# A hand-ordered kernel for linear attention and a feed-forward block: a new order of steps, more transposes by DMA, wider warm matmuls

## The chip, the cores and the metric

The kernel runs on one core of one Trainium2 chip. The metric is the device time of one execution in microseconds; lower is better. Before the change it is 157.49 us, the median of three runs (156.46 to 158.19).

## What is computed

The first part is linear attention with a decaying state, for 4 batches, 8 heads, 768 positions and head dimension 48. Its output, 384 wide, is the input x of the second part: a normalisation over the 384 columns, a matmul to 1536, a relu, a matmul back to 384, and x added.

```python
def _attn_ref(r, k, v, w, u):
    ...
    for t in range(S):
        kt, vt, rt = (k[:, :, t].copy(), v[:, :, t].copy(), r[:, :, t].copy())
        cur = np.einsum('bhd,bhe->bhde', u[None] * kt, vt)
        y[:, :, t] = np.einsum('bhd,bhde->bhe', rt, state + cur)
        state = w[None, :, :, None] * state + np.einsum('bhd,bhe->bhde', kt, vt)

def _moe_ref(x, g_ln, w_ch1, w_ch2):
    mu = np.mean(x, axis=-1, keepdims=True)
    var = np.mean((x - mu) ** 2, axis=-1, keepdims=True)
    xn = (x - mu) / np.sqrt(var + 1e-06) * g_ln
    ch = np.maximum(xn @ w_ch1, 0.0) @ w_ch2
    return (x + ch).astype(np.float32)
```

All inputs and the output are float32.

## The kernel before

The work is cut into 24 chunks of 128 positions (6 for each batch); chunks of one batch hand a state Z on from one to the next. Every piece of work on a chunk is a small function with a short name, and a table written out in the source, PLAN, lists some 1,100 steps in the form name, index, engine (v for VectorE, DVE; s for ScalarE, ACT; g for GpSimd, POOL). The program calls them in the order of the table. No scheduler moves anything: each engine executes its own steps in the table's order, and a step that waits holds everything behind it on its engine. The SyncE queue (SP) is such an order, too. It issues nearly all DMAs, and one that waits for its data or for a free buffer holds all later ones.

The steps of the start-up:

- WF loads the row w, LG the gains; LN, WBM (a matmul that spreads the row), FK and FR make the decay factors Fk and Fr of keys and rows from it. ROWSI issues four small loads of u and w from ACT's queue; UW (POOL) and WL (ACT) make from them what S and ZU need.
- MW and MP fill constants and the padding of key and row tiles, on DVE.
- LW1 n loads a third of the first weight matrix (768 KB), SW i scales a ninth of it into bf16 (three steps for each third), IW2 n loads a third of the second matrix; it is issued by POOL.
- WU and DU are matmuls on a zero tile that compute nothing; their index is how many.

The steps of chunk i:

- LK, LR, LV load keys, rows (r) and values, 192 KB each, in ten buffers each. SK and SR multiply keys and rows by their factors, CV casts the values.
- TR transposes scaled rows and keys on PE, eight transposes, into the PSUM tile `tr`, which has one buffer; TC (or TCr and TCk) copies them out. In TKD a DMA turns the keys, in TRD the rows; then TR has four transposes, or isn't there.
- AT makes the attention scores, AM (or AMa and AMb) multiplies them by the mask on DVE. Q multiplies turned rows and keys for the diagonal. S makes the diagonal sums and the chunk's contribution to the state, CC copies the sums out, ZU and ZD update the state, VB multiplies values by the sums, Y makes the output of the attention in PSUM, and X adds both to x on DVE.
- SQ and XN give square sums and the centred x, RS the factor of the normalisation. LT transposes xn on PE into `tr` and XT copies it out; for later chunks LTD does both by DMA.

Chunks 0 to 7 and 20 to 23 enter the feed-forward part alone, chunks 8 to 19 in pairs (GROUPS). UP of index 16 g + m makes up to 512 columns of the hidden layer of group g, RL is its relu, DN of index 4 i + d adds a third of the second matmul of chunk i, OT adds x, STO stores. The last chunk is done in halves (DA, DB, OA, OB, SA, SB).

Of the kernel before, what the change touches and what calls it, by code (L numbers as in the profile page):

```python
# [92 lines left out]
def kernel(  # L93
# [105 lines left out]

    def times(e, out, in0, in1):  # L200
        engines[e].tensor_tensor(out=out, in0=in0, in1=in1, op=ALU.mult)  # L201
# [429 lines left out]
```

## Time and profile before

| What | Value |
|---|---|
| Median of three runs | 157.49 us |
| Span of the profiled execution, first to last instruction | 153.7 us |
| TensorE (PE), busy | 143.1 us, 93% |
| VectorE (DVE), busy | 106.4 us, 69% |
| ScalarE (ACT), busy | 88.7 us, 58% |
| GpSimd (POOL), busy | 87.5 us, 57% |
| DMA packets, bytes | 93142, 25.53 MB |
| of these packets, under 512 B | 88385 |
| HBM read and written | 18.88 MB, 4.72 MB |

The profiled execution's own time is known by its span; the 3.8 us between 153.7 and the median of the runs lie around it (start and end of the program). In a row of the timeline the first two numbers are the start and the length in us; in a group of instructions, the numbers behind the bar are busy time in us, mean duration in ns, and the idle time of the engine before them with what ended it. PE counts as busy while its pipeline drains, so a PE that is 93% busy can still start its matmuls late.

### The profile page before, as it was taken

What the parts mean: (1) busy time and instruction counts of PE and PEld (TensorE: products, weight loads), DVE (VectorE), ACT (ScalarE), POOL (GpSimd) and SP (SyncE); (2) the same over time, 40 slices, a digit from 0 to 9 for tenths busy, and PEclk for the clock granted to TensorE, in tenths of its full rate; (3) what the DMA queues carried; (4) which work ended last, traced back from release to release, by engine and by line L of the source; (5) the groups of instructions that cost most, each with busy time, mean ns of one, the idle gap of its engine ahead of it and who ended that gap; (6) DMA issues with size and microseconds to landing.
All of it is one profiled execution on the core that took longest, in us unless ns stands there. A gap on an engine that the chain in (4) does not pass through costs nothing.

```text
span 153.7 us, 4643 instructions
## 1 busy us (share of the span) xinstructions
PE 143.1 (93%) x1866; PEld 115.1 (75%) x1866; DVE 106.4 (69%) x220; ACT 88.7 (58%) x190; POOL 87.5 (57%) x126
## 2 busy tenths in 40 slices
PE   7989696999999999899999999999999999899991
PEld 4877585877786788688678769688787887568880
DVE  3399785655998886958884969997887454455121
ACT  4424794436648857667868657638577444144440
POOL 3437697422575897485932899573843969431100
PEclk9999999999999999999999999999999999999999
DMA  3999999949999897989988999595353754212211
GB/s 48 212 214 353 208 306 211 200 108 219 226 198 246 167 230 164 209 168 214 231 198 174 258 201 187 109 188 115 81 152 85 123 163 114 53 51 78 80 51 51
DMA packets 93142, 25.53 MB, mean 166 GB/s; under 512 B 88385, under 2 KB 91586, under 8 KB 93122
## 3 DMA queue, kind: packets, MB, share of 16 engines
q1 hardware_dynamic: 91858, 24.06, 71.2%
q0 software_dynamic: 432, 1.18, 3.9%
q8 instruction: 14, 0.23, 0.6%
q10 hardware_dynamic: 832, 0.00, 0.3%
q14 instruction: 6, 0.05, 0.1%
HBM read 18.88 MB, written 4.72 MB: 154 GB/s over the span
## 4 chain that ended last, share of the span: by engine, by line
PE 54%; DMA 21%; DVE 9%; SPq 6%; issue 3%; POOL 3%; ACT 1%; DVEq 0%; ACTq 0%; POOLq 0%
PE o L527 22%; PE hp L499 21%; DMA kf<-in_k_dram 11%; DMA w_sb<-in_moe_w_ch_dram 4%; DVE A L365 3%; DMA vf<-in_v_dram 3%; DMA xT<-xn 3%; PE at L355 2%; PE tr L336 2%; SPq L320 2%; POOL Vb L418 2%; PE y L436 2%; SPq L317 2%; PE s L399 1%; PE y L428 1%
## 5 line engine op out<-in xcount | busy, mean ns | idle before, releaser
L515 ACT ACTIVATE hT<-hp 128x512 bf16<-128x512 f32 x70 | 41.2, 596 | 32.2 <-PE hp L499 31.1
L499 PE MATMUL hp<-xT,w_sb 128*128 128x128 bf16 (+1 forms) x648 | 57.0, 237 | 1.6 <-DMA xT<-xn 0.8
L527 PE MATMUL o<-w_sb,hT 128*128 128x384 bf16 x276 | 53.9, 326 | 2.0 <-DMA w_sb<-in_moe_w_ch_dram 1.1
L499 PEld LDWEIGHTS <-w_sb 128*128 128x128 bf16 x648 | 49.0, 114 | 5.9 <-DMA xT<-xn 1.1
L527 PEld LDWEIGHTS <-hT 128*128 128x128 bf16 x276 | 24.8, 98 | 14.1 <-DMA w_sb<-in_moe_w_ch_dram 1.3
L365 DVE TENSOR_TENSOR A<-at,mask 128x1024 bf16<-128x1024 f32 (+1 forms) x26 | 29.4, 1135 | 0.9 <-PE at L355 0.7
L418 POOL TENSOR_TENSOR Vb<-vf,cc 128x384 f32<-128x384 f32 x24 | 20.2, 841 | 13.6 <-ACT cc L196 7.6
L583 DVE SCALAR_TENSOR_TENSOR ot<-o,rs,x 128x384 f32<-128x384 f32 x23 | 14.1, 613 | 16.8 <-PE o L527 14.6
L450 ACT ACTIVATE sqj<-x,sm 128x384 bf16<-128x384 f32 x24 | 14.7, 613 | 4.2 <-DVE x L443 3.9
L443 DVE SCALAR_TENSOR_TENSOR x<-y,Vb 128x384 f32<-128x384 f32 x24 | 13.2, 552 | 4.6 <-POOL Vb L418 2.7
L201 POOL TENSOR_TENSOR sck<-kf,Fk 128x384 bf16<-128x384 f32 x10 | 10.0, 1008 | 9.3 <-DMA kf<-in_k_dram 6.3
L201 POOL TENSOR_TENSOR scr<-rf,Fr 128x384 bf16<-128x384 f32 x9 | 9.8, 1091 | 8.8 <-DVE q L201 5.1
L201 POOL TENSOR_TENSOR q<-trs 128x512 bf16<-128x512 bf16 x9 | 10.9, 1215 | 6.7 <-DVE trs L198 4.0
L201 POOL TENSOR_TENSOR Z<-ZS,WLZ 128x384 bf16<-128x384 f32 x12 | 12.0, 1004 | 2.3 <-DVE ZS L412 2.3
L196 ACT COPY trs<-tr 128x1024 bf16<-128x1024 bf16 (+1 forms) x12 | 10.4, 866 | 3.2 <-PE tr L336 3.2
L201 DVE TENSOR_TENSOR sck<-kf,Fk 128x384 bf16<-128x384 f32 x14 | 8.1, 582 | 5.9 <-DMA kf<-in_k_dram 5.6
L201 DVE TENSOR_TENSOR q<-trs 128x512 bf16<-128x512 bf16 x15 | 9.1, 604 | 4.2 <-ACT trs L196 3.3
L467 POOL TENSOR_TENSOR rs<-rs,expo 128x1 f32<-128x1 f32 (+1 forms) x18 | 10.8, 602 | 1.5
L355 PE MATMUL at<-trs 48*128 48x128 bf16 x192 | 9.5, 218 | 0.5 <-DVE trs L198 0.4
L201 DVE TENSOR_TENSOR scr<-rf,Fr 128x384 bf16<-128x384 f32 x15 | 8.8, 599 | 1.8 <-DMA rf<-in_r_dram 1.6
L196 ACT CAST vv<-vf 128x384 bf16<-128x384 f32 x16 | 8.2, 510 | 3.1 <-DMA vf<-in_v_dram 2.3
L259 PE MATMUL o<-warm 128*128 128x128 bf16 x94 | 8.9, 261 | 1.0 <-DVE warm L224 1.0
(72 smaller groups left out, 176.2 us busy)
## 6 DMA issues: line engine op xcount, KB each, us to landing
rf<-in_r_dram SPq DMA_DIRECT2D x24, 192.0 KB, 3.7
kf<-in_k_dram SPq DMA_DIRECT2D x24, 192.0 KB, 4.0
vf<-in_v_dram SPq DMA_DIRECT2D x24, 192.0 KB, 3.8
out_dram<-ot SPq DMA_DIRECT2D x23, 192.0 KB, 2.1
w_f<-in_moe_w_ch_dram SPq DMA_DIRECT2D x3, 768.0 KB, 6.5
w_sb<-in_moe_w_ch_dram POOLq DMA_DIRECT2D x3, 384.0 KB, 7.9
out_dram<-ot SPq DMA_DIRECT2D x2, 96.0 KB, 1.6
trs<-sck SPq DMA_TRANSPOSE x10, 2.9
```

The source lines that it names most:

```text
L196: nc.scalar.copy(out=out, in_=in_)
L201: engines[e].tensor_tensor(out=out, in0=in0, in1=in1, op=ALU.mult)
L355: nc.tensor.matmul(out=t[:, par, q, :], lhsT=trs(i)[p0 : p0 + D, 1, q, :], rhs=trs(i)[p0 : p0 + D, 0, q, :], start=True, stop=True,)
L365: nc.vector.tensor_tensor(out=AA(i)[:, a:b].rearrange("p e q t -> p (e q) t"), in0=psum["at", i][:, a:b].rearrange("p e q t -> p (e q) t") ...
L418: nc.gpsimd.tensor_tensor(out=Vb(i)[:].rearrange("p (h d) -> p h d", h=H), in0=vf(i)[:], in1=cc(i)[:].unsqueeze(2).to_broadcast([P, H, D]) ...
L443: nc.vector.scalar_tensor_tensor(out=xx(i)[:], in0=psum["y", i][:, :C], scalar=1.0, in1=Vb(i)[:], op0=ALU.mult, op1=ALU.add, accum_out=sm[ ...
L450: nc.scalar.activation(out=sqj[:], in_=xx(i)[:], func=ACT.Square, bias=sm[i][:], scale=-float(C), accum_out=sq[g][:, j : j + 1])
L467: nc.gpsimd.tensor_tensor(out=rs[g][:], in0=rs[g][:], in1=expo[:, :n], op=ALU.pow)
L499: nc.tensor.matmul(out=t[:, a * gw : (a + 1) * gw], lhsT=w1_sb[n][kc][:, fb::FB], rhs=xT(g)[:, kc, :gw], start=(kc == 0), stop=(kc == CK - 1),
L515: nc.scalar.activation(out=o, in_=s, func=ACT.Relu)
L527: nc.tensor.matmul(out=psum["o", i][:, :C], lhsT=hT(g)[:, fk, j * P : (j + 1) * P], rhs=w2_sb[d][:, a, :], start=(fk == 0), stop=(fk == FK ...
L583: nc.vector.scalar_tensor_tensor(out=ot(i)[:], in0=psum["o", i][:, :C], scalar=rs[g][:, j : j + 1], in1=xx(i)[:], op0=ALU.mult, op1=ALU.add,)
```

## The change

The table PLAN is replaced as a whole. Order, engines and the number of DU matmuls are new. Keys are turned by DMA from chunk 12 on (before 14), r from chunk 18 (before 20), xn from chunk 12 (before 14). VB and ZD take their engine from the table (before always POOL). WU and DU use one matmul of 512 columns for four of 128, by reading the zero tile four times. Stores can be issued by ACT, which this table doesn't use.

By the tables, these counts change (v, s, g):

| Step | Before | After |
|---|---|---|
| RL | v 2, s 70 | v 20, s 52 |
| VB | g 24 | v 8, g 16 |
| ZD | g 12 | v 7, g 5 |
| Q | v 15, g 9 | v 18, g 6 |
| SK | v 14, g 10 | v 11, g 13 |
| SR | v 15, g 9 | v 12, g 12 |
| XN | v 8, s 12, g 4 | v 4, s 14, g 6 |
| CV | v 3, s 16, g 5 | v 5, s 14, g 5 |
| SW | v 3, s 4, g 2 | v 2, s 6, g 1 |
| TKD, TRD, LTD | 10, 4, 10 | 12, 6, 12 |
| WU and DU, in 128 columns | 94 | 105 |

```diff
-K_BY_DMA = [14, 15, 16, 17, 18, 19, 20, 21, 22, 23]
+K_BY_DMA = [12, 13, 14, 15, 16, 17, 18, 19, 20, 21, 22, 23]
...
 PLAN = """
-MW,0,v WF,0,- TL,0,s MI,0,g WU,13,- MM,0,g MP,0,v LN,0,s LG,0,- ROWSI,0,s WBM,0,- LR,0,-
-UGC,0,s FK,0,s LK,0,- FR,0,s LR,1,- SR,0,g WL,0,s SK,0,v LK,1,- UW,0,g DU,24,- TR,0,-
-SR,1,v LK,2,- TCk,0,v SK,1,v LV,0,- TCr,0,v SK,2,v DU,12,- AT,0,- LR,2,- TR,1,- CV,0,s
-AMa,0,v LV,1,- Q,0,g AMb,0,v SR,2,v LW1,0,- DU,7,- Y,0,- S,0,- TCk,1,v CC,0,s TCr,1,v
-CV,1,s ZU,0,v Q,1,g DU,10,- TR,2,- LV,2,- TC,2,v DU,4,- AT,1,- VB,0,g S,1,- SW,2,s
-AMa,1,v LW1,1,- SW,1,g SW,0,s X,0,v Q,2,v CV,2,g XN,0,s AMb,1,v DU,20,- LT,0,- CC,1,v
-SQ,0,s Y,1,- ZU,1,v LK,3,- VB,1,g AT,2,- XT,0,v SW,5,s SW,4,v RS,0,g UP,0,- LR,3,-
-X,1,v SW,3,s AM,2,v S,2,- SK,3,g XN,1,s LW1,2,- UP,1,- RL,0,s SR,3,v LT,1,- IW2,0,g
-SQ,1,s Y,2,- XT,1,v IW2,1,g RL,1,s CC,2,v DU,1,- TR,3,- ZU,2,v VB,2,g UP,17,- LV,3,-
-TC,3,s SW,8,g UP,16,- X,2,v RL,17,s SW,7,v IW2,2,g AT,3,- SW,6,v RL,16,s CV,3,g Q,3,v
-DU,3,- UP,18,- SQ,2,s XN,2,g UP,2,- AM,3,v RS,2,g RL,18,s LT,2,- DN,0,- RS,1,g XT,2,v
-S,3,- RL,2,s UP,34,- CC,3,v VB,3,g Y,3,- RL,34,s ZU,3,v UP,32,- DN,1,- X,3,v UP,33,-
...
+MW,0,v TL,0,s MM,0,g LK,0,- WU,13,- DU,32,- MI,0,g LV,0,- LG,0,- WF,0,- LV,1,- LR,0,- LK,1,- LK,3,- LN,0,s WBM,0,-
+DU,20,- LR,1,- LK,2,- FR,0,s LW1,1,- FK,0,s SR,0,v LR,2,- ROWSI,0,s MP,0,v SK,0,g LW1,2,- TR,0,- DU,8,- SR,1,v SK,1,v
+CV,1,s LR,3,- TCk,0,v UGC,0,s TCr,0,s Q,0,v TR,1,- AT,0,- DU,8,- TCk,1,v CV,0,v LV,2,- AMa,0,v WL,0,s UW,0,g LW1,0,-
+SR,2,v SW,5,s S,0,- DU,16,- AMb,0,v SW,4,g LV,3,- TCr,1,s CC,0,v SK,2,g SK,3,v LK,4,- SW,8,s ZU,0,v LR,4,- Q,1,v
+SW,6,v S,1,- VB,0,v Y,0,- TR,2,- CC,1,s SW,3,s SR,3,g X,0,v AT,1,- DU,8,- TC,2,s AMb,1,v CV,2,g AMa,1,v XN,0,s
+VB,1,g LK,5,- ZU,1,v SW,1,s Y,1,- IW2,0,g Q,2,v LT,0,- X,1,v LR,5,- S,2,- IW2,1,g XT,0,v AT,2,- SW,0,v CC,2,s
+CV,3,s UP,1,- LV,4,- AM,2,v XN,1,g SW,2,s TR,3,- VB,2,g LR,6,- TC,3,s ZU,2,v Y,2,- SK,4,g LK,6,- UP,0,- X,2,v
+LT,1,- Q,3,v XN,2,s SR,4,v S,3,- RL,1,s XT,1,v AT,3,- RL,0,s LT,2,- SR,5,v UP,17,- SQ,0,s XT,2,v AM,3,v TR,4,-
+SQ,1,s RS,0,g UP,16,- RL,17,s SK,5,v IW2,2,g DN,0,- SW,7,s CC,3,v LK,7,- TC,4,v VB,3,g UP,32,- RL,16,v Y,3,- RL,32,s
+TR,5,- X,3,v UP,18,- LR,7,- Q,4,v SQ,3,s ZU,3,v CV,4,g AT,4,- TC,5,s LR,8,- UP,2,- AM,4,v SR,6,g S,4,- RL,18,s
...
+    def issuer(e):
+        return nc.scalar if e == "s" else nc.sync
...
     def WU(i, e):
         if not warm_ps:
             warm_ps.append(ps.tile([P, 512], FP32, name="o"))
-        for _ in range(i):
+        wide, rest = divmod(i, 4)
+        for _ in range(wide):
+            nc.tensor.matmul(
+                out=warm_ps[0][:], lhsT=warm[:], rhs=warm[:].unsqueeze(1).to_broadcast([P, 4, P]), start=True, stop=True
+            )
+        for _ in range(rest):
             nc.tensor.matmul(out=warm_ps[0][:, :P], lhsT=warm[:], rhs=warm[:], start=True, stop=True)
...
     def ZD(i, e):
-        times("g", ZZ(i)[:], ZS(i)[:], WLZ[:])
+        times(e, ZZ(i)[:], ZS(i)[:], WLZ[:])
 
     def VB(i, e):
-        nc.gpsimd.tensor_tensor(
+        engines[e].tensor_tensor(
             out=Vb(i)[:].rearrange("p (h d) -> p h d", h=H), in0=vf(i)[:],
             in1=cc(i)[:].unsqueeze(2).to_broadcast([P, H, D]), op=ALU.mult,
         )
...
     def STO(i, e):
         b, c = divmod(i, NCH)
-        nc.sync.dma_start(out=out[b, c * L : (c + 1) * L, :], in_=ot(i)[:])
+        issuer(e).dma_start(out=out[b, c * L : (c + 1) * L, :], in_=ot(i)[:])
```

In the new table the loads and DMA turns on SP begin LK 0, LV 0, LG 0, WF 0, LV 1, LR 0, LK 1, LK 3, LR 1, LK 2, LW1 1, LR 2, LW1 2, LR 3, LV 2, LW1 0, LV 3, LK 4, LR 4, LK 5, LR 5, LV 4, LR 6, LK 6, LK 7, LR 7, LR 8; the first store, STO 0, stands behind LR 9 (before behind LK 5). In the middle of the table TKD 12 stands behind LK 15, and LK 18 behind TKD 12.

## Prediction

> **What bounds the kernel now.** I read the engines' busy shares and the slices first, then the chain of waits, then the timeline of the first 30 us, then the groups by shape.
>
> ```profile
> span 153.7 us, 4643 instructions
> ...
> PE   7989696999999999899999999999999999899991
> ...
> DMA  3999999949999897989988999595353754212211
> ```
>
> TensorE (PE) is full from slice 8 on, the DMA engines until about 95 us. So two limits follow each other: arriving data, then PE's own work.
>
> ```profile
> 10.62 7.57 DMA kf<-in_k_dram
> 18.32 0.94 POOL sck L201
> 19.26 6.73 DMA w_sb<-in_moe_w_ch_dram
> 26.04 0.82 PE o L527 x4
> ...
> 63.92 4.95 DMA kf<-in_k_dram
> ...
> 128.88 3.89 DMA xT<-xn
> ```
>
> Columns: start, length. The start-up waits for keys 3, which hold POOL and thereby the issue of the first w2 block; DN 0 starts at 26.04. At 63.92 keys arrive late again, and at 128.88 one transposed row block.
>
> ```profile
> 1.03 1.57 PE L259 MATMUL o<-warm 128*128 128x128 bf16 x13 [1.03 <-DVE warm L224]
> 2.09 0.52 ACT L265 ACTIVATE ln_row<-w_row 1x384 f32<-1x384 f32 x1
> 2.10 0.93 ACTq L213 DMA_DIRECT2D u_p<-in_u_dram  x2
> 3.05 0.96 ACTq L213 DMA_DIRECT2D w_p<-in_w_dram  x2
> 4.24 2.74 PE L259 MATMUL o<-warm 128*128 128x128 bf16 x24
> 4.41 0.58 ACT L273 ACTIVATE Fk<-y,pow_i 128x384 f32<-128x384 f32 x1
> 13.80 1.28 PE L259 MATMUL o<-warm 128*128 128x128 bf16 x20
> 17.06 0.86 PE L499 MATMUL hp<-xT,w_sb 128*128 128x128 bf16 x12
> ```
>
> Row w arrives by 2.09, Fk starts at 4.41, the first UP at 17.06. A warm matmul of 128 columns costs 107 ns at first (24 start within 2.5 us) and 56 ns later (20 in 1.1).
>
> **My measure: lag.** From start to start PE spends 0.67 us on a single UP, 0.655 on a paired one, 0.65 on DN, 0.33 on half a DN, 0.22 on four transposes, 0.33 on AT, 0.17 on LT, 0.20 on Y and 0.10 on S, with 0.17 more on each for 20 chunks. With 36 single and 36 paired UP, 69 DN, 6 halves, 34 times four transposes, 24 AT, Y and S and 14 LT, all such work is 127.0 us before. Lag is the time minus the work done up to there; it can only grow, and each growth is a wait of PE (or a warm matmul): 16.4 at DN 0 (9.7 done), 23.3 at the last matmul's end (150.33). So the dense part loses 6.9: about 2.0 until 57 us, 3.1 from there to 82, 1.8 later. Behind PE lie 3.4 us of span, and 3.8 from the span to the runs' median (157.49).
>
> **The change, part by part.** *PE work.* Keys 12, 13 and rows 18, 19 leave PE (4 x 0.22), the normalised rows of 12 and 13 too (2 x 0.17): 1.2 off, 125.8 remain. The six DMA turns that replace them cost SP 1.2 us of issue each and land after 2.9. LTD stands further from its UP now (Y to UP: at least 8.5 us of PE work for chunks 12 to 22, against 4.4), and the turns of keys 12 and 13 have 5 us of PE work before AT, so I take 0; the shortest is keys 22 with 2.9. Uncovered, one costs what LTD 21 cost, 0.9. On SP, keys 18 and values and rows 16 queue behind TKD 12, which waits for SK 12; their users stand 15 us of PE work later.
>
> *Row w* goes from first to fourth on SP, behind keys 0 and values 0. The first load took 3.15 us to land (issued 1.61), each next one 0.9. So keys 0 land at 0.73 + 3.15 = 3.9 and values 0 at 4.8; I take row w at 4.4, between (3.6 if nothing delays it: fourth issue at 2.3, and the 1.36 it took before; 5.4 if both must land first), 2.3 late.
>
> *Warm matmuls* in 512 columns have the same columns: 105 times 128 against 94, 0.6 us more at 56 ns, under waits for data. But 45 of them now precede WBM: 1.03 + 45 x 0.107 = 5.85, then WBM 1.6 (two passes, as before). Fr and Fk run from 7.6 to 8.7, 3.2 late. Should PE speed up at 4.9 instead, they come 0.6 earlier, and the next load hides it.
>
> *ROWSI* moves behind Fk on ACT. Its four issues take 1.9 us there (2.10 to 4.01), now 8.7 to 10.6; CV 1, UGC and TCr 0 queue behind, so Q 0 starts at 11.9. The rows land 3.5 after the last issue, at 13.7: UW, so S 0, and WL, so ZU 0, wait for that.
>
> *DVE's start.* MP (0.9) now stands behind SR 0. SR 2 waits for rows 2, the ninth load, behind one w1 block; before, the same volume had landed at 14.76 (values 2), and the first load now goes out 0.8 earlier: 14.0. Then DVE runs without a pause: SR 2, AMb, CC, SK 3, ZU, Q 1 are 2.5; SW 6 needs the second w1 block (17.5 - 0.8 = 16.7); SW 6, VB 0, X 0, two masks, ZU 1, Q 2, X 1, XT 0 are 4.3. First UP at 21.0, where 4.2 of PE's work is done; before it was 17.06 at 3.8. Start-up lag grows from 13.3 to 16.8.
>
> *Loads against w2.* POOL reaches IW2 0 at 20.0 (rows 3, the tenth load, at 18.19 - 0.8 = 17.4; then SR 1.1, CV 0.7, VB 0.8). Before, packets followed the issue by 2.8 us, one block took 2.0, and while they ran the loads nearly stood: keys 4 landed at 24.31, the next load at 30.68. Twelve loads and three w1 blocks had landed by 22.23; now by 21.4, then keys 4 and rows 4 by 23.2. Blocks 0 and 1 run from 22.8 to 26.8 and leave keys 5 and rows 5 behind: 26.8 + 2 x 0.9 + 0.6 to land = 29.2. DVE has SR 5 ahead of XT 2, and TR 4 needs the PSUM bank that XT 2 frees: TR 4 at 30.1 instead of after UP 17 (26.0), with 8.1 done. **Lag 22.0**, 5.6 more than at DN 0 before. Low bound: loads keep half the queue, rows 5 at 26.9, lag 19.7; high: with 1.8 of a cold PE, 23.8. The third w2 block, behind RS 0 on POOL, goes out at 27 and lands by 35; DN 2 needs it at 16.8 + 22.0 = 38.8, so it costs nothing.
>
> *Engines.* Eighteen RL go to DVE, eight VB and seven ZD leave POOL for it.
>
> ```profile
> L515 ACT ACTIVATE hT<-hp 128x512 bf16<-128x512 f32 x70 | 41.2, 596 | 32.2 <-PE hp L499 31.1
> L517 DVE TENSOR_SCALAR hT<-hp 128x512 bf16<-128x512 f32 x2 | 1.4, 688 | 0.4 <-PE hp L499 0.4
> L418 POOL TENSOR_TENSOR Vb<-vf,cc 128x384 f32<-128x384 f32 x24 | 20.2, 841 | 13.6 <-ACT cc L196 7.6 <-DVE cc L198 5.9
> L201 DVE TENSOR_TENSOR sck<-kf,Fk 128x384 bf16<-128x384 f32 x14 | 8.1, 582 | 5.9 <-DMA kf<-in_k_dram 5.6
> ```
>
> Start to start a RL on DVE is 0.61; VB and ZD there are unseen, nearest is SK, 0.47 (bounds: 0.41, the fastest xn, and 1.2, the slowest SR). Summed so (mask 1.14, OT 0.53, X 0.48, ZU 0.46, Q 0.43, RL on ACT 0.49, VB 0.79 and ZD 0.96 on POOL), DVE goes from 98 to 111 us, ACT from 76 to 69, POOL from 82 to 72. From X 3 to X 8 DVE has 23.3 us against 24.8 of PE work; before, against 30.7. DVE is nearly a second bound there. Both engines wait for each other in turn (AT, mask, Y, x, LT, UP), but the mask stands 2 to 5 us ahead of its Y as before; so I keep the early loss of 2.0. [...] In this trace 13 of 14 SK on DVE take about 0.55, also under POOL's work, and one 0.99. [...]
>
> *The middle* improves. The first store stood behind keys 5 and held SP for 4.3 us; it now follows rows 9. Keys 12 landed at 68.87 when 49.9 of PE work preceded their use (69.0 - 49.9 = 19, the lag itself). The new order asks for the loads nearly in order of use; after rows 5 the tightest is rows 7, at 35.5 for 16.9 of work: 18.6, under 22.0. Of 3.1 I keep 0.5, of the late 1.8 0.9.
>
> Sum: 125.8 + 22.0 + 3.4 = 151.2; + 3.4 = span 154.6; + 3.8 = **158.4 us**, 0.6% over the median. A difference under about 1% can't be told from none here.
>
> **Rivals.** *Faster (0.27):* the loads pass w2, lag 19.7, dense loss 2.5: 125.8 + 19.7 + 2.5 + 7.2 = 155.2. For it: the distances are longer everywhere; against: 24.31 to 30.68.
>
> *Slower, DVE decides (0.23):* DVE has only 6% to spare from X 3 to X 8, and in 84 to 100 us, its fullest, it was 91% busy. At 80% it needs 29.1 for that stretch and 23.1 for 18.5 until X 13 (22.0 of PE work): 4.3 + 1.1 in place of 2.0. It gives 161.8, and decides once DVE falls under 94%.
>
> *Slower, cold PE (0.10):* PE would stand 4 us before TR 4; the longest stand before the first DN was 1.3 and cost no speed. At 107 ns for as long as at the start (7.2 us) half of that is lost, 3.6; between 0 and 3.6 I price 1.8: 160.2. [...]
>
> **Chances.** Forecast 0.40, its own range 157.0 to 160.0 (three quarters within 1%, the rest slower). Faster 0.27 is the first rival; same 0.30 + 0.02 of the cold PE; slower 0.10 + 0.23 + 0.08. The range reaches from 153.8 (lag 19.5 with a dense loss of 1.3) to 162.5, into both sides.
>
> **What would show it.** Fk near 8.1, first UP near 21, TR 4 near 30 behind rows 5, two DN waits for keys gone at 60 to 78, no wait before UP 240. Wrong if the first UP comes before 19, if TR 4 doesn't wait, or if DVE idles little and PE still loses over 5 us after 30.

## The result and the profile after

The changed kernel takes 163.55 us (median of four runs, 162.53 to 165.78). The kernel before, run beside it, took 157.84. The ratio is 1.042, 95% interval 1.032 to 1.053: slower. The forecast was 158.4, its range 153.8 to 162.5, so the time lies above the range. Some executions of a kernel run more than a per cent slower than its others; the ratios leave these out, the medians do not. The profiled execution took 162.93 us for a span of 160.8, and its last matmul ends at 157.64 (before: 150.33).

The page of the changed kernel, busy tenths in 40 slices of 4.02 us:

```profile
span 160.8 us, 4461 instructions
...
PE   7828768499999999999999999989299999999992
...
PEclk9985899879999999999999999999959999999999
DMA  5999999998898999999687595989586404320412
```

The row PEclk was all nines before. Now it drops in slices 2 to 4 (counted from 0), again in 7 and 8, and in slice 29. The PE row has two holes: the start, and slice 28 (112.6 to 116.6 us). Around that second hole the DMA row still shows 5 to 9; before, PE had no such hole.

The chain of waits (start, length):

```profile
20.82 8.57 DMA rf<-in_r_dram
29.42 0.56 DVE scr L184
29.98 0.28 DVE xT L181
30.30 0.61 PE tr L327 x8
...
31.88 1.28 PE o L518 x4
...
103.77 3.96 DMA trs<-scr
...
110.54 2.44 DMA trs<-sck
...
113.77 2.70 DMA xT<-xn
...
116.61 1.44 PE hp L490 x6
118.05 1.28 PE o L518 x4
```

Two different things end last. At 29.42 rows 5 have landed, SR 5 and XT 2 follow, and TR 4 starts at 30.30: the start is as the forecast drew it. From 103.77 to 116.5 three DMA turns stand in the chain one after the other (TRD 19, TKD 20, LTD 17). The forecast had priced these at nothing. At 31.88 and from 116.61 the matmuls also take twice their usual 0.65 us.

The timeline of the start (start, length, engine, line):

```profile
6.55 0.57 ACT L264 ACTIVATE Fk<-y,pow_i 128x384 f32<-128x384 f32 x1
10.43 0.57 DVE L184 TENSOR_TENSOR scr<-rf,Fr 128x384 bf16<-128x384 f32 x1 [1.90 <-DMA rf<-in_r_dram]
11.39 0.41 DVE L181 COPY trs<-tr 128x512 bf16<-128x512 bf16 x1
12.47 0.58 PE L327 MATMUL tr<-ident,scr 128*128 128x128 bf16 x4 [3.07 <-ACT trs L179]
14.98 0.74 DVE L184 TENSOR_TENSOR scr<-rf,Fr 128x384 bf16<-128x384 f32 x1
17.59 1.22 DVE L297 TENSOR_SCALAR w_sb<-w_f,g_neg 128x512 bf16<-128x512 f32 x1
18.73 0.85 DVE L409 TENSOR_TENSOR Vb<-vf,cc 128x384 f32<-128x384 f32 x1
23.18 0.86 PE L490 MATMUL hp<-xT,w_sb 128*128 128x128 bf16 x12
```

Fk comes at 6.55, earlier than forecast, but DVE's SR 1 waits until 10.43 for rows 1, and TCk 0, TCr 0 and TR 1 stand behind it. SR 2 follows at 14.98, SW 6 at 17.59, and the first UP starts at 23.18.

The groups of the moved steps:

```profile
L506 ACT ACTIVATE hT<-hp 128x512 bf16<-128x512 f32 x52 | 30.5, 595 | 37.1 <-PE hp L490 36.7
L508 DVE TENSOR_SCALAR hT<-hp 128x512 bf16<-128x512 f32 x20 | 13.7, 687 | 6.6 <-PE hp L490 6.5
L409 DVE TENSOR_TENSOR Vb<-vf,cc 128x384 f32<-128x384 f32 x8 | 5.2, 655 | 0.1
L184 DVE TENSOR_TENSOR sck<-kf,Fk 128x384 bf16<-128x384 f32 x11 | 6.1, 553 | 0.1
```

A VB takes 655 ns on DVE, 0.1 us more than SK, the row it had been priced by. DVE is 117.8 us busy, 73% of the span.

**Where the time went**, in the lag of the prediction (time minus PE work done, same prices per step), read from the profiles of before and after:

| Stretch | before | after | difference |
|---|---|---|---|
| Lag at TR 4 (after) or DN 0 (before) | 16.3 | 22.2 | +5.8 |
| From there to DN 4 | 0.0 | 2.0 | +2.0 |
| DN 4 to DN 44 | 4.7 | 1.4 | -3.3 |
| DN 44 to DN 64 ("late loss") | 0.6 | 5.8 | +5.2 |
| DN 64 to the last matmul | 1.7 | 0.5 | -1.2 |
| PE work | 127.0 | 125.8 | -1.2 |

They add up to the 7.3 us by which the last matmul comes later.

### The profile page after: what moved, and what is told of

The parts are those of the page before. It is cut to its first block, busy times and chain, and to the rows that moved or that the text cites. A ratio compares the mean times of both kernels' runs of the same rounds, so it can differ in the third digit from the quotient of the medians.

```text
span 160.8 us, 4461 instructions
## 1 busy us (share of the span) xinstructions
PE 144.2 (90%) x1777; PEld 110.6 (69%) x1777; DVE 117.8 (73%) x244; ACT 79.2 (49%) x173; POOL 77.3 (48%) x115
## 3 DMA queue, kind: packets, MB, share of 16 engines
q0 software_dynamic: 432, 1.18, 4.0%
## 4 chain that ended last, share of the span: by engine, by line
PE 72%; DMA 14%; SPq 9%; issue 1%; DVE 1%; ACT 0%; DVEq 0%
PE hp L490 28%; PE o L518 27%; DMA rf<-in_r_dram 8%; PE at L346 4%; PE tr L327 3%; PE y L427 3%; DMA trs<-scr 2%; SPq L308 2%; SPq L305 2%; PE y L419 2%; SPq L311 2%; SPq L288 2%; PE s L390 2%; DMA xT<-xn 2%; DMA trs<-sck 2%
## 5 line engine op out<-in xcount | busy, mean ns | idle before, releaser
L490 PE MATMUL hp<-xT,w_sb 128*128 128x128 bf16 (+1 forms) x648 | 59.9, 241 | 1.6 <-DMA xT<-xn 1.6
L518 PE MATMUL o<-w_sb,hT 128*128 128x384 bf16 x276 | 57.2, 332 | 1.5 <-DVE ot L574 1.5
L506 ACT ACTIVATE hT<-hp 128x512 bf16<-128x512 f32 x52 | 30.5, 595 | 37.1 <-PE hp L490 36.7
L518 PEld LDWEIGHTS <-hT 128*128 128x128 bf16 x276 | 24.8, 99 | 12.6 <-issue 2.3
L184 POOL TENSOR_TENSOR sck<-kf,Fk 128x384 bf16<-128x384 f32 x13 | 13.8, 1063 | 15.0 <-ACT Fk L264 5.2
L409 POOL TENSOR_TENSOR Vb<-vf,cc 128x384 f32<-128x384 f32 x16 | 14.0, 878 | 10.4 <-DVE cc L181 10.4
L508 DVE TENSOR_SCALAR hT<-hp 128x512 bf16<-128x512 f32 x20 | 13.7, 687 | 6.6 <-PE hp L490 6.5
L455 POOL TENSOR_SCALAR rs<-sq 128x1 f32<-128x1 f32 (+1 forms) x18 | 4.2, 232 | 20.8 <-ACT sqj L441 19.9
L327 PE MATMUL tr<-ident,scr 128*128 128x128 bf16 x72 | 7.2, 223 | 5.9 <-ACT trs L179 3.1
L447 ACT ACTIVATE xn<-x,sm 128x384 bf16<-128x384 f32 x14 | 8.6, 617 | 6.2 <-DVE x L434 6.0
L449 POOL TENSOR_SCALAR xn<-x,sm 128x384 bf16<-128x384 f32 x6 | 3.5, 585 | 15.7 <-DVE x L434 10.9
```

The costliest lines, as they stand in the source:

```text
L327: nc.tensor.transpose(out=t[:, a * HP + q, :], in_=flat[:, q, :], identity=ident[:])
L409: engines[e].tensor_tensor(out=Vb(i)[:].rearrange("p (h d) -> p h d", h=H), in0=vf(i)[:], in1=cc(i)[:].unsqueeze(2).to_broadcast([P, H, D] ...
L490: nc.tensor.matmul(out=t[:, a * gw : (a + 1) * gw], lhsT=w1_sb[n][kc][:, fb::FB], rhs=xT(g)[:, kc, :gw], start=(kc == 0), stop=(kc == CK - 1),
L506: nc.scalar.activation(out=o, in_=s, func=ACT.Relu)
L508: nc.vector.tensor_relu(out=o, in_=s)
L518: nc.tensor.matmul(out=psum["o", i][:, :C], lhsT=hT(g)[:, fk, j * P : (j + 1) * P], rhs=w2_sb[d][:, a, :], start=(fk == 0), stop=(fk == FK ...
```

## The experiments

In the tables and texts below, lag and late loss come from each kernel's own profile. A ratio is to the kernel before, measured on the same chip beside the experiment. The changed kernel's ratio is 1.042.

| Run | Lag at TR 4 | at DN 4 | at DN 44 | late loss | lag at the end | ratio, interval |
|---|---|---|---|---|---|---|
| changed kernel | 22.2 | 24.2 | 25.6 | 5.8 | 31.9 | 1.042, 1.032 to 1.053 |
| e8_before_six_turns | 17.3 | 17.3 | 25.1 | 6.8 | 32.7 | 1.038, 1.030 to 1.046 |
| e4_turns_back | 21.9 | 22.3 | 25.0 | 1.1 | 26.6 | 1.029, 1.021 to 1.037 |
| e18_four_back | 21.9 | 22.3 | 24.5 | 3.7 | 28.7 | 1.039, 1.024 to 1.055 |
| e19_two_back | 22.2 | 25.2 | 26.6 | 1.3 | 28.4 | 1.028, 1.012 to 1.044 |
| e3_stores_act | 22.7 | 23.1 | 24.5 | 5.0 | 30.0 | 1.033, 1.011 to 1.054 |
| e5_loads_behind | 22.7 | 24.7 | 26.1 | 5.6 | 32.2 | 1.048, 1.032 to 1.063 |
| e9_loads_and_stores | 22.1 | 22.5 | 23.9 | 3.6 | 28.0 | 1.025, 1.014 to 1.036 |
| e14_split_loads | 22.1 | 22.5 | 23.9 | 11.6 | 36.0 | 1.079, 1.068 to 1.090 |
| e15_quarter_loads | 22.6 | 24.6 | 26.0 | 2.1 | 28.6 | 1.012, 1.000 to 1.024 |
| e6_relu_back | 25.0 | 26.4 | 28.9 | 4.6 | 34.0 | 1.049, 1.035 to 1.064 |
| e1_xt2_first | 21.6 | 23.6 | 26.4 | 5.1 | 32.0 | 1.046, 1.035 to 1.056 |
| e2_warm_tr4 | 22.3 | 22.6 | 24.0 | 4.6 | 29.1 | 1.036, 1.026 to 1.046 |
| e7_start_order | 23.1 | 24.8 | 26.1 | 6.8 | 33.4 | 1.042, 1.032 to 1.052 |
| e12_rows1_early | 19.9 | 22.3 | 23.7 | 6.8 | 31.0 | 1.041, 1.032 to 1.049 |
| e13_rows5_off_path | 19.6 | 21.1 | 24.7 | 0.6 | 25.8 | 1.017, 1.009 to 1.026 |
| e10_start_of_before | 16.7 | 16.7 | 28.3 | 3.4 | 32.2 | 1.040, 1.027 to 1.053 |
| e11_best_guess | 16.5 | 16.5 | 26.8 | 0.9 | 28.2 | 1.038, 1.029 to 1.047 |

PE work is 125.8 us, except 126.2 in e19_two_back, 126.6 in e18_four_back, and 127.0 in e4, e11 and e13 (0.22 for each row or key turned on PE, 0.17 for each LT). The tables' lag for e18 and e19 counts that work as done.

Each lag comes from one execution, so it has a spread. e1, e2, e7 and e12 leave the late part as it is in the changed kernel, and their late losses are 5.1, 4.6, 6.8 and 6.8 beside its 5.8. A late loss between 4.6 and 6.8 therefore can't be told from the changed kernel's.

### The six DMA turns

**e8_before_six_turns: the six turns alone.** In the kernel before:

```diff
-K_BY_DMA = [14, 15, ...
+K_BY_DMA = [12, 13, 14, 15, ...
-... TC,12,s ... TC,13,s ... LT,12,- XT,12,s ... LT,13,- XT,13,v ... TR,18,- TCr,18,v ... TR,19,- TCr,19,v
+... TKD,12,- TCr,12,s ... TKD,13,- TCr,13,s ... LTD,12,- ... LTD,13,- ... TRD,18,- ... TRD,19,-
```

> The kernel before, with the six DMA turns of the change alone: keys 12 and 13, normalised rows 12 and 13, rows 18 and 19 by DMA. Theory A (what costs is turns together with many loads in SP's queue; in the kernel before SP has 4 us of idle time between 82 and 104 us and its loads are done by 106): PE's work falls by 1.2 us, waits grow by 0 to 2 us, the time is within 1.2 us of before. Rival B (six more turns by themselves cost 3.5 us or more, as taking them back from the changed kernel gained): 2.5 to 4 us slower than before. The forecast's own term (turns cost nothing): 1.2 us faster.

It became 3.8% slower (by the ratio; the medians of all runs are 162.86 and 158.44), more than either theory allowed. Lag goes from 17.3 to 25.1 by DN 44 (before: 16.4 to 21.0) and loses another 6.8 to DN 64 (before: 0.6). The turns of the normalised rows stand in the chain. So the six turns by themselves cost about what the whole change costs; theory A's "0 to 2 us" fails, and rival B's size is nearer, though a little small.

**e4_turns_back, e18_four_back, e19_two_back: which of them.** In the changed kernel, e4 puts all six back, e18 the four of chunks 12 and 13, e19 the two of rows 18 and 19:

```diff
-TRD,18,-            ... TRD,19,-
+TR,18,- TCr,18,s    ... TR,19,- TCr,19,s      (e4, e19)
-TKD,12,- TCr,12,s   ... LTD,12,-
+TC,12,s             ... LT,12,- XT,12,s       (e4, e18; chunk 13 alike)
```

> The six turns that the change gave to DMA (keys 12 and 13, normalised rows 12 and 13, rows 18 and 19) go back to PE with their copies on ACT and DVE. PE has 1.2 us more work. Theory A (SP's issue time): SP gets 7.4 us back, the loss from 102 to 120 falls from 5.6 to under 2, and the time falls by 2.5 to 4 us net. Rival B (the DMA turns cost nothing, as the forecast said, and the loss is DVE's): 1.2 us slower, or up to 2 with the copies.

> Keys 12 and 13 and the normalised rows 12 and 13 go back to PE, TRD 18 and TRD 19 stay on SP: 0.8 us more PE work, some 5 us less of SP's time between 64 and 89 us. Theory A (SP never catches up between 64 and 120 us, so time taken there early is still missing at 104): most of the gain of e4_turns_back comes with these four, the loss from 102 to 124 us falls under 2.5 and the time by 2 to 3 us against the changed kernel. Rival B (only what stands right ahead of the late turns counts): loss still 4 us or more, the time within 1 us.

> Rows 18 and 19 alone go back to PE: 0.4 us more PE work, 2.5 us less of SP's time between 95 and 105 us. Theory A: the gain is in proportion to SP's time, a third of that of e4_turns_back in lag, the loss falls from 5.6 to about 4 us and the time by 1 us. Rival B: these two are what holds TKD 20 and LTD 17; the loss falls under 2.5 us and the time by 2.5 to 3.5 us.

The late loss falls from 5.8 to 1.1 with all six back, to 3.7 with four, and to 1.3 with the two of rows 18 and 19 alone. The intervals of the times overlap each other's, so here the profile decides. 1.1 and 1.3 lie far outside the spread of 4.6 to 6.8. So the two row turns, at 95.89 and 103.77 us in the changed kernel, make most of the late loss, as rival B of e19 has it: without them it falls by 4.5, and taking all six back adds only 0.2 to that. (The time gained, some 2.2 us by the ratios, is a little under the 2.5 to 3.5 of that rival.) The 3.7 of e18 lies only 0.9 under the spread, and its profile lacks the half-speed stretch that costs the changed kernel 1.4 there, so it is not shown that time which SP saves early reaches the late part. Theory A, that all SP time counts alike, does not fit: it wanted under 2.5 for e18 and about 4 for e19.

**What makes turns late.** The SP queue of the changed kernel around the loss (start, length of the issue), and the data that two of these turns wait to move:

```profile
106.70 0.53 SPq L581 DMA_DIRECT2D out_dram<-ot  x1
107.28 0.42 SPq L311 DMA_DIRECT2D vf<-in_v_dram  x1
107.76 0.78 SPq L308 DMA_DIRECT2D rf<-in_r_dram  x1
108.70 1.74 SPq L470 DMA_TRANSPOSE trs<-scr  x1
110.54 1.21 SPq L466 DMA_TRANSPOSE trs<-sck  x1
111.85 1.20 SPq L462 DMA_TRANSPOSE xT<-xn  x1
113.11 0.57 SPq L305 DMA_DIRECT2D kf<-in_k_dram  x1
113.77 1.21 SPq L462 DMA_TRANSPOSE xT<-xn  x1
```

```profile
102.39 0.55 DVE L184 TENSOR_TENSOR sck<-kf,Fk 128x384 bf16<-128x384 f32 x1
...
105.38 0.41 DVE L449 TENSOR_SCALAR xn<-x,sm 128x384 bf16<-128x384 f32 x1
```

Keys 20 are ready at 102.94 and their turn (L466) goes out at 110.54. The normalised rows of chunk 17 are ready at 105.79 and LTD 17, the second L462, goes out at 113.77. Between these rows SP pauses for 0.16 us at most; summed over its rows (pauses over 0.06 us), it stands idle for 4.6 us in all from 64 to 120 us (7.3 before). So the keys are held for 7.6 us after they are ready, the rows of chunk 17 for 8.0. Q 20 then waits 2.8 us on DVE for TKD 20, OT 13 stands behind Q 20, and DN 56 waits 1.45 us for the PSUM bank that OT 13 frees; UP 192 waits 1.59 us for LTD 17; then PE runs at half speed for 3.4 us, which costs another 1.4 (UP 192 1.44 instead of 0.66, DN 57 1.28 instead of 0.65).

**e3_stores_act, e5_loads_behind, e9_loads_and_stores: the others in the queue.**

```diff
-STO,4,- ... STO,14,-
+STO,4,s ... STO,14,s                                   (e3, e9)
-... LV,23,- ... LR,22,- ... LV,22,- ... LR,23,- ... LTD,16,- ... LK,23,- ... LTD,17,- ...
+... LTD,16,- ... LTD,17,- LR,22,- LR,23,- LV,22,- ... TRD,21,- LK,23,- ... STO,13,- LV,23,-   (e5, e9)
-... SR,22,g ... SR,23,g ... RS,12,g
+... RS,12,g SR,22,g SR,23,g                             (e5, e9)
```

> Stores 4 to 14 are issued by ACT instead of SP. Theory A (between 64 and 120 us SP issues without a pause, so turns go out after their data are ready, and this makes the 5.6 us that PE loses from 102 to 120): SP gets some 6.5 us back, TRD 19 and TKD 20 go out 3 to 6 us earlier against PE's work, the loss falls under 2.5 us and the time falls by 3 to 4 us. Rival B (DVE or the turns' own transfer time make that loss): the time changes by less than 1 us. Rival C (ACT's RL are held by the issues, 0.5 to 0.9 us each): up to 2 us slower.

> Five late loads on SP (rows 22 and 23, values 22 and 23, keys 23) that stand ahead of LTD 16, LTD 17, TRD 20 or TKD 20 go behind LTD 17, with SR 22 and SR 23 behind RS 12 on POOL; the number of loads and turns is the same. Theory A (turns are late because loads that nobody needs yet stand ahead of them in SP's one queue: 0.6 us of issue and 0.9 us of transfer each): LTD 17 goes out 3 us or more earlier against PE's work, the loss from 102 to 120 us falls from about 5 to under 2, the time falls by 3 to 5 us. Rival B (the loss is the number of turns, or DVE): within 1 us of the time after. Rival C (the loads come too late for their own users instead): the loss moves to 120 to 135 us, no gain.

> The edits of e5_loads_behind and e3_stores_act together: five late loads go behind LTD 17, and ACT issues stores 4 to 14. Theory A (turns, late loads and stores stand in one queue on SP; whoever is put ahead makes the next one late, which is why each edit by itself gained little: with the loads moved, OT 14 waited for store 11 instead): both waits are gone, PE loses under 1.5 us from 102 to 124 us in place of 5 to 6, and the time falls by 4 to 5.5 us against the changed kernel. Rival B (the late work has one more limit, the transfers themselves): the wait moves on again, and the time falls by less than 2.5 us.

Each edit alone leaves a late loss, 5.0 and 5.6, that can't be told from 5.8. In e5 LTD 17 does go out earlier, and the waits from 107 to 117 us are gone. But now store 11 stands behind loads and a turn, and OT 14, which reuses its buffer, waits for it; PE stands for 3.5 us. The chain of e5:

```profile
115.63 0.58 SPq L311
116.26 3.27 DMA out_dram<-ot
119.62 0.63 DVE ot L574
```

With both edits (e9) the loss up to DN 60 is 0.7, and then the next one in the queue is late: TKD 21, issued behind two loads of values, needs 5.13 us to land and costs 2.9 us. The chain of e9:

```profile
112.50 1.24 SPq L311
113.79 5.13 DMA trs<-sck
```

So theory A of e3 and of e5, each a single edit, failed; e9's theory A was right about the two waits and rival B about the next one. Here a new order in the full queue mostly chose who is late: e9 still loses 3.6. With eleven stores on ACT's queue (e3) the late loss is 5.0 us against 5.8, inside the spread; whether ACT's queue moved their bytes beside SP's or in their place no run shows.

**e14_split_loads and e15_quarter_loads: issue or transfer.**

```diff
+        for a, b in ((0, H // 2), (H // 2, H)) if i >= 18 else ((0, H),):          (e14)
+            nc.sync.dma_start(out=kf(i)[:, a:b], in_=chunk_src(k, i)[:, a:b])
+        n = H // 4 if i >= 18 else H                                               (e15)
+        nc.sync.dma_start(out=kf(i)[:, :n], in_=chunk_src(k, i)[:, :n])
```

> Each of the 18 loads of chunks 18 to 23 is issued as two halves: the same bytes, twice the issues on SP, some 6 to 10 us more of SP's time between 66 and 120 us. Theory A (SP's issue time makes the turns late): the loss from 102 to 124 us grows by 4 us or more, the time is 167 us or more. Rival B (the transfers ahead in the queue do): within 1.5 us of the changed kernel, 162 to 165 us.

> Each of the 18 loads of chunks 18 to 23 brings only the first two of its eight heads (the other six keep what the buffer held): the same issues, some 12 us less of transfer. Theory A (SP's issue time): the loss from 102 to 124 us stays above 4 us, the time within 1.5 us of the changed kernel. Rival B (transfers): the loss falls under 2 us, the time by 3.5 to 5 us, to 158 to 160 us.

Both ends count. Eighteen more issues for the same bytes double the late loss, from 5.8 to 11.6, and the time goes to a ratio of 1.079. (PE runs at half speed for 6.8 us in this stretch, so a part of the 11.6 is the clock's.) A quarter of the bytes in the same number of loads (six of eight heads are left out) brings it down to 2.1 and the ratio to 1.012, near e15's rival B (its profile is of the longest of its four executions, 159.58 us). Both intervals lie apart from the changed kernel's. The windows of the changed kernel and of e15 show the second one (busy us and instructions by engine, then PEclk, DMA share, GB/s):

```profile
104.00:120.00 16.00, 12.50 (x109) 9.07 (x108) 9.48 (x19) 5.02 (x12) 7.40 (x10) 0.89 0.82 163
```

```profile
104.00:120.00 16.00, 15.07 (x151) 11.46 (x150) 12.16 (x25) 6.92 (x15) 7.60 (x10) 1.00 0.53 128
```

PE works 15.07 of 16 us instead of 12.50 once the DMA share falls from 0.82 to 0.53. With less to move, issues were shorter there too: turns issued from 104 to 122 us take 1.18 to 1.22 us each in e15, and up to 1.74 in the changed kernel. From LK 15 to LTD 17 all of SP's issues sum to 45.4 us in the changed kernel, to 50.6 in e14 and to 41.4 in e15. So e15, too, gave SP issue time back: in these runs SP's issue time and the backlog of transfers are one limit, seen at two ends. Whether it is the bytes or the number of packets, which fall together in e15, no run tells.

### The start

**e1_xt2_first and e2_warm_tr4: the stand before TR 4.**

```diff
-LT,2,- SR,5,v UP,17,- SQ,0,s XT,2,v AM,3,v TR,4,-
+LT,2,- UP,17,- SQ,0,s XT,2,v SR,5,v AM,3,v TR,4,-           (e1)
+LT,2,- SR,5,v UP,17,- SQ,0,s XT,2,v AM,3,v DU,40,- TR,4,-   (e2)
```

> SR 5 moves behind XT 2 on DVE; nothing else changes. Theory A (the stand of 2.1 us before TR 4, and the low granted clock that follows it, cost about 4.5 us together): TR 4 starts near 28.0 instead of 30.30, UP 16, DN 0 and UP 32 take nearer 0.7 us than 1.1 to 1.5, and the time falls by 2.3 (the stand alone) to 4.5 us. Rival B (rows 5 are needed a moment later anyway, by TR 5 and the mask of chunk 3 that follow SR 5 on DVE): the stand moves from TR 4 to the next step, and the time changes by less than 1 us.

> Ten warm matmuls of 512 columns (2.1 us at full speed) are put before TR 4, where PE stands for 2.1 us. Theory A (the clock falls because PE stands): TR 4 still starts near 30.3, but the matmuls behind it run at their usual 0.65 to 0.7 us per step, and the 2.3 us lost from 30 to 36 us shrink to under 1: the time falls by 1.5 to 2.3 us. Rival B (PE is slow there for another reason, such as waits for RL or the third w2 block): no change, or up to 0.5 us slower.

In e1 the stand is gone and the clock stays up, but the profiled start happened to be slow (first UP at 24.84 instead of 23.18), and TR 5 waited until 33.89 for what rows 5 hold up (SR 5 at 31.00): the lag at DN 4 is 23.6 and the time within its uncertainty of the changed kernel's. Rival B. In e2 lag grows by 0.3 from TR 4 to DN 4 instead of 2.0, as theory A wants. It is not proof by itself, though: e3, e4 and e9, which left that place alone, lost only 0.4. The granted clock tells why. In the windows (length, then busy us of PE first; PEclk is the third last number) of the changed kernel and of e9:

```profile
27.69:31.10 3.41, 1.33 (x25) 1.21 (x23) 1.68 (x3) 2.26 (x6) 1.35 (x3) 1.00 1.04 197
31.11:34.52 3.41, 3.41 (x29) 2.72 (x27) 2.00 (x5) 0.05 (x1) 2.25 (x3) 0.50 1.05 201
```

```profile
24.90:28.31 3.41, 2.06 (x36) 1.53 (x34) 1.08 (x4) 3.33 (x9) 1.01 (x3) 1.00 1.15 224
28.31:31.72 3.41, 1.50 (x23) 1.37 (x23) 2.38 (x5) 0.65 (x2) 0.34 (x1) 1.00 1.08 197
31.73:35.14 3.41, 3.41 (x65) 3.10 (x64) 3.15 (x9) 1.78 (x4) 2.26 (x3) 1.00 1.12 223
```

After stands of 2.1 to 3.5 us before TR 4 (LT 2 in e6) the clock fell to 0.50 in six profiles (changed kernel, e5, e6, e7, e15, e19), for 3.4 us in five and for 6.8 in e19, and not in two (e9 and e14, both 3.0 us). After stands of 1.5 to 1.7 it did not fall in any of three (e3, e4, e18). Where it fell it cost 1.4 to 3.0 us, elsewhere 0.3 to 0.4. The length of the stand alone does not decide: in the records of all 20 profiles here the granted clock changes only at the ends of windows of 3.41 us, which lie elsewhere in each execution. Every stretch at 1.00 or 0.50 between two changes is a whole number of them. Of the windows at 1.00 in which PE was busy for less than 0.41 of the time, all 28 were followed by one at 0.50; of 731 in which it was busy for 0.61 or more, none; of the 18 between, four. The changed kernel's stand fell into one window, with PE busy for 1.33 of 3.41 us; e9's longer stand was split over two, with 2.06 and 1.50. The warm matmuls of e2 fill such a window, and its granted clock is 1.00 from 20 to 40 us. The window before the changed kernel's drop was not idle: 1.33 us of work in it did not keep the clock up.

**e7_start_order and e12_rows1_early: row w, or rows 1.**

```diff
-LK,0,- ... LV,0,- LG,0,- WF,0,- LV,1,- LR,0,- LK,1,- LK,3,- LN,0,s WBM,0,- DU,20,- LR,1,- ... ROWSI,0,s MP,0,v
+WF,0,- LK,0,- ... MP,0,v LN,0,s ROWSI,0,s WBM,0,- DU,32,- ...                     (e7, e12)
+LG,0,- LR,0,- LK,1,- LR,1,- LV,0,- LK,2,- LV,1,- LK,3,- ... XT,2,v SR,5,v          (e12 as well)
```

> Row w goes first on SP again, LN, the four row loads of ACT, the memsets (MP) and WBM follow at once, and the 32 warm matmuls stand behind WBM. Theory A (TR 4 waits for rows 5, which the w2 blocks hold back, as the forecast had it): first UP near 20.5 instead of 23.2, but TR 4 still at 29.5 to 30.5, and the time falls by less than 1 us. Rival B (the start's chain through row w, Fr, the rows u and w sets the rest): TR 4 and all that follows 2.5 us earlier, and the time too.

> e7_start_order, and keys 1 and rows 1 are loaded before values 0, values 1 and keys 3, and SR 5 stands behind XT 2 on DVE. Theory A (in the changed kernel DVE's SR 1 waits until 10.4 us for rows 1, the ninth load, and TCk 0, TCr 0 and TR 1 stand behind it; that, not row w, holds the start): rows 1 land near 8, TR 1 starts near 10 in place of 12.4, PE's clock falls less, the first UP starts at 20 to 21.5 in place of 23 to 24, TR 4 near 28 instead of 30 to 31, and the time falls by 2 to 3 us. Rival B (the loads up to rows 5 and the w2 blocks set it): the first UP comes earlier, but TR 5 or UP 16 waits for the same arrivals and the time is within 1 us of the changed kernel.

With row w first again nothing came earlier (first UP at 24.09, TR 4 at 31.20): SK 0, which needs Fk, started at 5.47 in place of 7.20, but TR 1 still started at 12.44, since SR 1 still waited for rows 1. Rival B is out. Theory A's earlier first UP did not come either, only its outcome, no gain: the delay of row w was idle. With rows 1 loaded earlier (e12), TR 1 comes at 11.38 and TR 4 at 28.01, but the first UP still at 23.42: now SR 2 waits on DVE until 14.62 for rows 2, Q 1 and S 1 come behind it, PE stands from 13.99 to 17.30, and its clock is at 0.50 from 16.4 to 23.2 us. TR 5 then starts only at 32.46, behind rows 5 (SR 5 on DVE at 29.58, then the mask, SK 5 and TC 4). Lag at DN 4 is 22.3, the value of e4 and near e9's 22.5, whose start was untouched: rival B of e12.

**e13_rows5_off_path: rows 5 out of the way.** The start of e12, the late part of e11, and:

```diff
-... UP,32,- ... TR,5,- X,3,v UP,18,- ... Q,4,v ... AT,4,- TC,5,s ... UP,2,- ...
+... UP,32,- ... X,3,v UP,18,- ... Q,4,v SR,5,v SK,5,v ... AT,4,- ... UP,2,- TR,5,- TC,5,s ...
```

> The start of e12_rows1_early, and the steps that need rows and keys 5 (SR 5, SK 5, TR 5, TC 5) stand behind UP 18, AT 4 and UP 2, so that PE has 2 us of other work when rows 5 land; six turns on PE and stores 4 to 14 on ACT as in e11_best_guess. Theory A (rows 5 set the start's lag; e12_rows1_early had 19.9 at TR 4 and lost 2.0 at TR 5): lag at DN 4 is 20 to 20.8 in place of 22.3, the late part loses 2 as in e11_best_guess, lag at the end is 23 to 24 with 127.0 of work, the time is 155 to 157.5 us, no slower than before. Rival B (the chains of chunks 4 and 5 then come late themselves): lag at DN 4 is 22 again and the time 158 to 160 us.

The timeline of e12 and that of e13 at this place:

```profile
29.78 0.83 PE L490 MATMUL hp<-xT,w_sb 128*128 128x128 bf16 x12
32.46 0.38 PE L327 MATMUL tr<-ident,scr 128*128 128x128 bf16 x4 [0.76 <-DVE trs L181]
```

```profile
29.49 0.83 PE L490 MATMUL hp<-xT,w_sb 128*128 128x128 bf16 x12
30.53 0.84 PE L490 MATMUL hp<-xT,w_sb 128*128 128x128 bf16 x12
31.64 0.86 PE L490 MATMUL hp<-xT,w_sb 128*128 128x128 bf16 x12
32.34 0.39 PE L327 MATMUL tr<-ident,scr 128*128 128x128 bf16 x4
```

Two UP now fill what was a wait, in which lag grew by 1.6 us. Lag at DN 4 is 21.1, the lowest that the changed order reached, but not the 20 to 20.8 of theory A. So of e12's 22.3, waiting for rows 5 is worth some 1.2, by one profile each; what sets the other 4.7 over the 16.4 of before no run shows (PE stands here, too, from 13.89 to 17.59 us before S 1). And 3.6 us were lost from DN 4 to DN 44 in place of 1.4: part of the gain is waited for later. At 158.28 us it is the fastest correction of the changed kernel, and still 1.7% slower than before.

**e10_start_of_before and e11_best_guess.** The order of before up to DN 4, then what the changed order has left; e11 with the turns of e4 and the stores of e3 besides.

> The order of the kernel before up to DN 4, then the order of the changed kernel with what is left (UP 49, RL 48 to 50, DN 5 and DN 6 put among the steps of chunks 4 and 5). Theory A (a start that is later is carried to the end one for one): lag at DN 4 is 16.4 in place of 24.2, and some of it comes back as waits for loads in the middle, since the forecast's tightest load, keys 12, wants a lag of 19; the end comes 3 to 5.5 us earlier. Rival B (the middle of the changed order waits for nothing only because it starts late; its loads are the bound): lag is back at 24 by DN 36, and the time falls by less than 1.5 us.

> e10_start_of_before with the six turns back on PE and ACT issuing stores 4 to 14. Theory A (start and SP's late queue are two separate losses that add): 4 to 5 us faster than e10_start_of_before, 153 to 156 us, faster than before by 1 to 3%. Rival B (one hides the other): within 2 us of e10_start_of_before.

Lag is 16.7 at DN 4 and 25.8 at DN 8. The chain there runs over TR, AT and masks of chunks 4 to 8: the joined order had no UP and DN left to put between them. So e10 shows an artefact of the joint and does not settle what a better start would be worth. e11 against e10 has a late loss of 0.9 instead of 3.4, but the medians differ by only 0.7 us (161.65 and 162.37). That is far from the 153 to 156 us of theory A and within the 2 us of rival B, but with the artefact in both runs it says little of the two losses.

### The engines

**e6_relu_back.** All RL on ACT, all VB and ZD on POOL.

```diff
-RL,...,v   VB,...,v   ZD,...,v      (35 steps)
+RL,...,s   VB,...,g   ZD,...,g
```

> All RL go back to ACT and all VB and ZD to POOL (35 steps leave DVE), the order stays. Theory A (DVE is not what costs the time; it still stands idle a quarter of the span): within 1 us of the time after, or slower where VB and ZD take 0.8 and 1.0 us on POOL in place of 0.55. Rival B (DVE is nearly a second bound, as the forecast had it in its second rival): the stretch from 36 to 102 us loses under 1 us in place of some 3, the time falls by 2 to 3 us.

Slower, not faster, from DN 4 to DN 44: 2.5 us lost instead of 1.4. (Its start was late as well, 25.0 at TR 4.) DVE was not a bound, and the forecast's second rival is out: taking the steps off DVE gained nothing. That having them on DVE helps is not shown, since e1 with an unchanged middle lost 2.8 there and the intervals of the ratios overlap.

**e17_before_stores_act.** The kernel before with stores 0 to 22 on ACT's queue.

> The kernel before, with stores 0 to 22 issued by ACT. Theory A (the middle of the kernel before loses 3 us because stores hold SP's queue: store 0 held it for 4.3 us, and keys 12 and 13 land late at 69): lag from DN 12 to DN 36 grows by under 2 us in place of 3.9, the time falls by 1.5 to 3 us. Rival B (the loads are late by their volume, not by the queue): within 1 us of before. Rival C (ACT is held at the stores, and its RL with it): 1 us or more slower.

The ratio is 1.019 (1.009 to 1.028), and lag from DN 12 to DN 36 grows by 4.9 in place of 3.9. No gain, rather a loss, which is the outcome of rival C; and keys 12, which land at 69.60 (before 68.87), were not late because of the stores. That ACT's RL are what loses is not shown: the chain of this run holds a store's landing (75.91, 4.43 us) for which OT waits.

## Why the prediction was wrong

The predicted lag at the end was 25.4, the measured one 31.9. By its own steps:

- **PE work**, 125.8: right in its difference. The prices listed add up to 126.3 for the kernel before, not 127.0; the rest are its four matmuls that carry a state over to the next chunk, at 0.17 each, which the working left unnamed.
- **Row w, Fk, ROWSI.** Fk was put at 8.1 and came at 6.55, since PE sped up within the first warm matmuls (those of 512 columns start 0.43 us apart until 3.7 us, 0.22 from 4.0 on): the two passes of WBM took 0.84 us, not 1.6. The whole term was idle anyway: e7 took the delay away and gained nothing. What held TR 1 was rows 1, the ninth load instead of the fifth (landed at 10.40, before at 7.15), with TCk 0 behind SR 1 on DVE. But e12 brought TR 1 forward by 1.1 us and not the first UP, so neither row w nor rows 1 sets the start alone. The working had Q 0 at 11.9 (it came at 12.45) for the wrong reason.
- **First UP at 21**, measured 23.18. DVE did run without a pause, as drawn, but SR 2 began at 14.98 instead of 14.0, behind the copies that waited for TR 1. And SW 6 to XT 0 took 5.4 us instead of 4.3 (SW 6 1.22, VB 0.85); why these were slow, no run shows. It did not move TR 4.
- **TR 4 at 30.1 behind rows 5 at 29.2**, measured 30.30 and 29.39. Right, and as far as the packets show for its reason. IW2 0 went out at 20.22 (forecast 20.0), and the packets of w2 blocks 0 and 1 ran from 22.56 to 28.36 us. From 23 to 27 us SP's queue moved only 47 to 232 packets a us, against 1,100 to 1,400 around; keys 5 and rows 5, issued at 20.07 and 20.82, landed at 28.66 and 29.39. No run moved the w2 blocks, so the packets alone speak for them as the cause. The lag was forecast as 22.0 and measured as 22.2, with the drop of the clock after it priced apart.
- **Cold PE**, a rival at 0.10 priced at 1.8 us and left out of the sum. It happened and cost 2.0 us at TR 4, and again 1.4 at 116 us. In five profiles of the same start (e3, e4, e9, e14, e18) the first of these did not happen. But each of the changed kernel's four executions has a mean granted clock of 0.948 to 0.967, which makes 10.6 to 17 us at half speed; the runs of the kernel before have 0.986 to 1.00.
- **The middle.** Both waits for keys are gone, and DN 4 to DN 44 loses 1.4 us where 2.5 was forecast. VB on DVE took 0.1 us more than the row of SK. The working split the 6.9 of before into 2.0, 3.1 and 1.8; by the starts of the steps it is 1.4, 2.7 and 2.9, so more of it was late than it took.
- **The DMA turns.** This is the step that failed. The working named 1.2 us of issue for each and the distance from each turn to its own user, took 0, and bounded one at 0.9. The distances were right. But it never added up SP: six turns are 7.2 us by its own price (8.9 as issued in the changed kernel), on a queue that in the profile of before stood idle for 7.3 us between 64 and 120. It also asked only what queues behind TKD 12, not behind TRD 18 and TRD 19. SP then held LTD 17 for 8.0 us and TKD 20 for 7.6 after their data were ready. The late part lost 6.3 us (5.8 and 0.5; 1.4 of it the clock) where 0.9 was kept. In the kernel before, the same six turns alone cost 3.8%; taking two of them back from the changed kernel brings the late loss from 5.8 to 1.3.
- **Around the span** 3.8 us were added, 2.1 measured. The 3.8 compared the span of one short execution with the median of three runs; the executions since have about 1.8 to 2.5 between span and time. So the 3.8 do not lie around the span, and that error of 1.7 hid a part of the miss by luck: the span is off by 6.2 us, the time by 5.2.

In sum: 0.2 at TR 4, 2.0 for the clock, -1.1 in the middle and 5.4 late make the 6.5 us of missing lag.

What stays open: why e1 and e13 lose 1.4 and 2.2 us more between DN 4 and DN 44 than the changed kernel, how much of e8's loss before DN 44 belongs to each of its turns, and what sets the start's lag besides rows 5.

## What to carry to other kernels

Before a transfer takes work from a busy engine, add up the queue it goes to, issue time and bytes, over the stretch where it will stand, beside the distance from each transfer to its user: the turns of rows 18 and 19, priced at 0 by that distance, made 4.5 of the 5.8 us of late loss (e19) through what was issued behind them. In a full queue a reorder may only choose who is late next (here turn, then store, then turn again, and e9 still lost 3.6 us); fewer entries (e19, 1.3) or fewer bytes (e15, 2.1) helped. In a start-up, find the load that the first engine in order waits for before pricing anything that only moves earlier work.

## What the hardware showed that was not expected

- A stand of PE of 2.1 us was enough, in some executions, to halve the granted clock for 3.4 us afterwards (6.8 in e19; 1.4 to 3.0 us lost); stands of 3.0 us left it at 1.00 in two others (e9, e14). The drops went with how busy PE was in a window of 3.41 us: under 0.41 of it the clock fell 28 times of 28, from 0.61 on never in 731.
- The issue of a DMA turn on SP took 1.18 to 1.23 us for 20 of the changed kernel's 30 turns, 1.26 to 2.02 for the other ten, and 2.8 for LTD 14 in e19. With 18 loads issued as two halves each (e14), the same bytes, the late loss grew by 5.8 us, a part of it the clock's.
- Ten of the eleven stores moved to ACT's queue in e3 took 0.34 to 0.41 us of issue there and one 1.04, against 0.36 to 1.4 on SP. The late loss was 5.0 us beside 5.8, inside the spread.
